# First blocks' exponents from bf16 parts, log a by two loads, and PSUM banks given by hand in a Mamba-2 + ELU kernel

## Chip, cores and metric

One core of a Trainium2 chip runs the whole program in one launch. The metric is the device time in microseconds (us). Before the change it is 388.47 us (median of three runs, 387.79 to 389.34). The profiled execution, from which the trace is read, took 387.49 us, with a span of 385.5 us from the first to the last instruction and a granted TensorE clock of 1.0.

## The reference, cut to what matters

```python
# x (4, 8, 768, 32), a (4, 8, 768), B and C (4, 8, 768, 16): batch, heads, sequence, ...
log_a = np.log(np.clip(a, 1e-06, 1.0))
for c in range(nc):                                  # chunks of 32 along the sequence
    cum = np.cumsum(la, axis=-1)
    L = np.exp(cum[:, :, :, None] - cum[:, :, None, :]) * causal
    M = np.einsum('bhin,bhjn->bhij', Cc, Bc) * L
    y_intra = np.einsum('bhij,bhjd->bhid', M, xc)
    y_inter = np.einsum('bhin,bhnd->bhid', Cc, state) * np.exp(cum)[:, :, :, None]
    y[:, :, sl] = y_intra + y_inter
    Bx = (Bc x xc) * np.exp(cum[:, :, -1:] - cum)    # outer product, cut
    state = np.exp(np.sum(la, axis=-1)) * state + np.sum(Bx, axis=2)

h = x @ w_in                                         # x: y as (3072, 256); w_in (256, 2048)
g = np.where(h > 0.0, h, np.exp(np.minimum(h, 0.0)) - 1.0)
out = g @ w_out                                      # w_out (2048, 256)
```

The weights arrive as 64-bit floats and are turned into 32-bit ones on the chip.

## The kernel before

The kernel takes the sequence in chunks of Q = 64 and works on 12 blocks n = 0 to 11 of 256 positions of one batch. Block 0 and block 1 are the first ones of two batches; from block 4 on two blocks are handled together. For each block the steps are: `turn` (transposes of B and C), `scores` (C times B), the decay L, `weigh` (M = scores times L), `sums` and `states` (the state at each chunk), `across` and `inside` (the two parts of y, copied to yT). Then come eight steps `l1` (y times w_in, two column groups each), each with an `elu`, and eight steps `l2` (times w_out). An fp32 matmul is done in two passes, so one l1 or l2 step is eight passes of 256 columns.

Loads and the exponents of all blocks; rows of `la` are those of block group g = 0, 1, 2 and 0 again:

```python
la = const.tile([P, 2, P], F32, name="la")
for k, g in enumerate((0, 1, 2, 0)):
    (nc.scalar if k % 2 else nc.sync).dma_start(out=la[BH * k:BH * (k + 1)], in_=...)
...
nc.vector.tensor_scalar(out=la, in0=la, scalar1=1e-6, scalar2=1.0, op0=ALU.max, op1=ALU.min)
nc.scalar.activation(la, la, ACT.Ln)
nc.vector.tensor_tensor_scan(out=F[:, 0]..., data0=keep..., data1=la..., ...)   # cum
nc.scalar.activation(F[:, 1], F[:, 0], ACT.Exp)
nc.vector.tensor_tensor(out=E..., in0=<last cum of the chunk>, in1=F_uv, op=ALU.subtract)
nc.scalar.activation(E, E, ACT.Exp)
```

For blocks 0 and 1 the exponent cum[i] - cum[j] is made in PSUM by TensorE: a bf16 product gives the causal mask (`first_low`), fp32 products with 32 rows each add cum[i] (`first_cum`) and subtract cum[j] (`first_minus`), and one exp reads the bank (`first_decay`). Later blocks get cum spread by a DMA through DRAM, and the exp takes -cum as its bias (`decay`), with the mask on GpSimd afterwards.

PSUM has eight banks. Seven are one pool, from which each new tile takes a free one; the eighth is used by the output of l2 and, early, by others:

```python
p_a = ctx.enter_context(tc.tile_pool(name="ps_a", bufs=7, space=PSUM))
p_o = ctx.enter_context(tc.tile_pool(name="ps_o", bufs=1, space=PSUM))
```

A piece of weights (256 columns of two groups) goes through `w_abs` and `w_low` (ScalarE or VectorE), `w_sign`, `w_high_a`, `w_high_b` (VectorE) and `w_sum` (GpSimd). `elu` is two activations and one VectorE operation that frees the bank:

```python
def elu():
    n, i, ps = lag.pop(0)
    nc.scalar.activation(e, ps, ACT.Relu, scale=-1.0)
    nc.scalar.activation(e, e, ACT.Exp, scale=-1.0)
    nc.vector.scalar_tensor_tensor(out=g_of[n][...], in0=e, scalar=1.0, in1=ps,
                                   op0=ALU.subtract, op1=ALU.max)
```

The order at the start and around block 1's end (each engine runs its own part in this order):

```python
first_low(0, 0); first_low(0, 1); idle_products(3); first_cum(*first)
eb = turned(E, "eb", 1.0, nc.scalar); turn(0); first_exp(0); scaled(0, nc.gpsimd); turn_exp(0)
sums(0, pool=p_o, tag="o"); first_minus(*first)
w_abs(0); first_decay(0, 0); w_low(0, nc.scalar); first_decay(0, 1); states(0)
scores(0); w_sign(0); w_high(0); w_sum(0)
for q in range(4): weigh(0, q)
first_low(1, 0); first_low(1, 1, p_o); w_abs(1); w_low(1, nc.scalar)
inside(across(0), 0)
...                                             # second and third piece
l1(0, 0); ...; first_cum(*second); first_minus(*second); l1(0, 1); elu(); ...
first_decay(1, 0); first_decay(1, 1); turn(1); ...; l1(0, 2); elu(); scores(1); sums(1, ...)
...; elu(); states(1); ...; l1(0, 3); w_take(4, nc.vector)
inside(across(1), 1)
ncum = turned(F[0:ROWS, 0], "ncum", -1.0, nc.vector)
w_give(4); elu(); load_bc(3)
for s, (n, i) in enumerate(((1, 0), (1, 1), (0, 4), (1, 2), (0, 5), (1, 3), (0, 6),
                            (1, 4), (0, 7), (1, 5), (1, 6), (1, 7))):
    l1(n, i)
    ...                                         # pieces; decay(2, s - 3) for s = 3 to 6; turn(2)
    if s == 7: scores(2); weigh(2, 0); weigh(2, 1)
    if s == 8: ...; weigh(2, 2); weigh(2, 3); sums(2, pool=p_o, tag="o"); states(2)
    if s == 10: inside(across(2), 2)
    if len(lag) > 1: elu()
```

In the rounds n = 3, 5, 7, 9 of the main loop (m = n + 1 is the pair that is prepared):

```python
for i in range(8):
    l2(n - 2, i); end_of_two(n, 2 * i); l1(n, i)
    while lag: elu()
    if i < 2: decay(m + 1, i + 2); scaled(m + i, nc.gpsimd)
    if i == 2: scores(m, m + 1); sums(m, m + 1); ...   # weigh and states of both
    end_of_two(n, 2 * i + 1)          # inside(across(m, m + 1), m, m + 1) where `ends` says
```

Of the kernel before, what the change touches and what calls it, by code (L numbers as in the profile page):

```python
# [28 lines left out]
def kernel(  # L29
# [33 lines left out]
    ROWS = NG * BH  # L63
# [12 lines left out]
    p_a = ctx.enter_context(tc.tile_pool(name="ps_a", bufs=7, space=PSUM))  # L76
    p_o = ctx.enter_context(tc.tile_pool(name="ps_o", bufs=1, space=PSUM))

    def psum(shape, name):
        return p_a.tile(shape, F32, tag="a", name=name)  # L80
# [6 lines left out]
    la = const.tile([P, 2, P], F32, name="la")  # L87
    for k, g in enumerate((0, 1, 2, 0)):
        (nc.scalar if k % 2 else nc.sync).dma_start(
            out=la[BH * k:BH * (k + 1)],  # L90
            in_=a.rearrange("b h (c s) -> (b h) c s", s=P)[:, 2 * g:2 * g + 2, :])

    nc.scalar.preload_act_table_set("natural_log_exp_and_others")
# [7 lines left out]
    def rows_of(n):  # L101
        b, g = place(n)
        return slice(BH * g + NH * b, BH * g + NH * (b + 1))

    def load_bc(n, c_queue=nc.sync):
        b, g = place(n)
        st.setdefault(n, {})["bc"] = raw.tile([P, 2, 2, NH, N], F32, tag="bc", name="bc")
        for u in range(2):
            sl = slice((2 * g + u) * P, (2 * g + u + 1) * P)
            for k, src in enumerate((B, C)):  # L110
                (nc.sync, c_queue)[k].dma_start(  # L111
                    out=st[n]["bc"][:, k, u], in_=src[b, :, sl, :].rearrange("h s n -> s h n"))
# [26 lines left out]
    def w_load(i):  # L139
        if i < len(pieces):  # L140
            w_raw[i] = conv.tile([P, 2, 2 * CW], U32, tag="w64", name="w64", bufs=W_AHEAD)
            nc.sync.dma_start(out=w_raw[i], in_=pieces[i][1])
# [5 lines left out]
    w_mag = {}  # L148

    def w_words(i):  # L150
        words = w_raw[i].rearrange("p k (f t) -> p k f t", t=2)
        return words[:, :, :, 0], words[:, :, :, 1]

    def w_abs(i):
        w_mag[i] = conv.tile([P, 2, CW], U32, tag="mag", name="mag")
        nc.scalar.activation(w_mag[i].bitcast(F32), w_words(i)[1].bitcast(F32), ACT.Abs)  # L156
# [4 lines left out]
    def w_low(i, eng):  # L161
        if eng is nc.scalar:
            eng.activation(pieces[i][0], w_words(i)[0], ACT.Identity, scale=2.0 ** -51, bias=two)
        else:
            eng.tensor_scalar(
                out=pieces[i][0], in0=w_words(i)[0], scalar1=2.0 ** -51, scalar2=2.0,
                op0=ALU.mult, op1=ALU.add)

    w_sgn = {}

    def w_sign(i):
        w_sgn[i] = conv.tile([P, 2, CW], U32, tag="sgn", name="sgn")
        nc.vector.tensor_scalar(
            out=w_sgn[i], in0=w_words(i)[1], scalar1=0x80000000, scalar2=None,
            op0=ALU.bitwise_and)

    def w_high_a(i):
        mag = w_mag[i]
# [3 lines left out]
            out=mag.bitcast(F32), in0=mag.bitcast(F32),  # L182
# [3 lines left out]
    def w_high_b(i, cols=slice(None)):  # L186
# [5 lines left out]
    def w_high(i):  # L192
        w_high_a(i)
        w_high_b(i)

    def w_sum(i, cols=slice(None)):
# [3 lines left out]
    load_bc(0, nc.scalar)  # L200
    load_x(0)
    w_load(0)
# [3 lines left out]
    idle = att.tile([P, 4, P], BF16, tag="M", name="idle", bufs=8)  # L206
    nc.vector.memset(idle, 0.0)
    ps_idle = p_o.tile([P, 4, P], F32, tag="o", name="ps_idle")

    def idle_products(count):  # L210
        for _ in range(count):
            nc.tensor.matmul(out=ps_idle, lhsT=idle[:, 0], rhs=idle, start=True, stop=True)

    idle_products(7)
# [11 lines left out]
    for v in range(2):  # L226
# [17 lines left out]
    minus = const.tile([P, P], F32, name="minus")  # L244
    nc.gpsimd.tensor_scalar(
        out=minus, in0=ident, scalar1=-1.0, scalar2=None, op0=ALU.mult)

    heads = [const.tile([ROWS, NH, N], F32, name=f"heads{n}") for n in range(3)]
    for n in range(3):
        nc.gpsimd.tensor_copy(  # L250
            heads[n], ident[0:ROWS, rows_of(n)].unsqueeze(2).to_broadcast([ROWS, NH, N]))


    nc.vector.tensor_scalar(out=la, in0=la, scalar1=1e-6, scalar2=1.0, op0=ALU.max, op1=ALU.min)
    nc.scalar.activation(la, la, ACT.Ln)

    F = const.tile([P, 2, 2, P], F32, name="F")
    nc.vector.tensor_tensor_scan(
        out=F[:, 0].rearrange("p c s -> p (c s)"), data0=keep.rearrange("p c s -> p (c s)"),
        data1=la.rearrange("p c s -> p (c s)"), initial=0.0, op0=ALU.mult, op1=ALU.add)  # L260
    nc.scalar.activation(F[:, 1], F[:, 0], ACT.Exp)

    E = const.tile([ROWS, 2, P], F32, name="E")
    F_uv = F[0:ROWS, 0].rearrange("r u (v i) -> r (u v) i", i=Q)
    nc.vector.tensor_tensor(
        out=E.rearrange("r u (v i) -> r (u v) i", i=Q),
        in0=F_uv[:, :, Q - 1:Q].to_broadcast([ROWS, 4, Q]), in1=F_uv, op=ALU.subtract)
    nc.scalar.activation(E, E, ACT.Exp)

# [3 lines left out]
    def write_flat():  # L273
        for v in range(2):
            nc.sync.dma_start(out=flat[v], in_=F[0:ROWS, 0, :, Q * v:Q * v + Q])
        nc.sync.dma_start(out=flat_exp, in_=F[0:ROWS, 1].rearrange("r u i -> r (u i)"))


    def turned(src, name, scale, eng):
        ps = psum([P, 2, ROWS], "ps_" + name)  # L280
        for u in range(2):
            nc.tensor.transpose(out=ps[:, u], in_=src[:, u], identity=ident[0:ROWS, 0:ROWS])
# [552 lines left out]
```

## Time and profile before

| | |
|---|---|
| time, median of 3 | 388.47 us |
| span of the profiled execution | 385.5 us |
| first l1 step starts | 13.68 us |
| last matmul ends | 382.5 us |
| passes of l1 and l2 (L538, L569, L585) | 768, 704 and 64 |
| moved by DMA | 25.15 MB, mean 65 GB/s |

PE is TensorE (PEld its weight loads), DVE VectorE, ACT ScalarE, POOL GpSimd, SP the engine that issues most loads. L538 is line 538 of the kernel: L538 is l1, L569 and L585 l2, L550, L551 and L552 the elu, L397 and L402 the decay, L417 scores, L426 weigh, L445 sums, L462 states, L490 across, L508 inside, L521 the copy to yT, L325 `scaled` (sc = B times eb), L368 and L379 the exponents of the first blocks. In a line of the timeline the first number is the start in us, the second the length of the group, then the operation, its output and inputs, how many instructions it has, and in brackets how long the engine had stood and who ended that. In the row of slices, each digit is the busy share of one fortieth of the span in tenths.

### The profile page before, as it was taken

How to read it: one execution, taken by the hardware profiler on the slowest of the kernel's cores; microseconds unless marked ns; L12 is line 12 of the kernel's file. 1: busy time of each engine (PE TensorE's matmuls, PEld its weight loads, DVE VectorE, ACT ScalarE, POOL GpSimd, SP SyncE). 2: the span in 40 equal slices, each digit the busy share in tenths (PEclk: the TensorE clock that was granted, in tenths of full speed). 3: DMA queues.
4: the chain of work that ended last, by engine and by line, in shares of the span. 5: the costliest groups of instructions: out<-in, count | busy, mean ns of one | idle time of the engine just before them, and what ended most of it. 6: DMA issues, size and time to landing. Idle time of an engine off the chain costs nothing.

```text
span 385.5 us, 8666 instructions
## 1 busy us (share of the span) xinstructions
PE 378.7 (98%) x3544; PEld 324.1 (84%) x3544; DVE 136.9 (36%) x280; ACT 196.7 (51%) x455; POOL 72.1 (19%) x131
## 2 busy tenths in 40 slices
PE   8899999999999999999999999999999999999996
PEld 4678788888888888888888888888888888888885
DVE  4877878932521232611132431123161212221000
ACT  3969969675334576344467335367534333334000
POOL 5525426623200112400022220011310000000000
PEclk9999999999999999999999999999999999999999
DMA  8979956543004505003524002540000000000000
GB/s 173 226 155 263 296 88 148 96 105 94 3 28 57 84 0 138 3 3 61 64 40 136 3 2 41 60 67 29 0 4 2 27 2 23 4 2 28 0 29 27
DMA packets 87176, 25.15 MB, mean 65 GB/s; under 512 B 77312, under 2 KB 81760, under 8 KB 87136
## 3 DMA queue, kind: packets, MB, share of 16 engines
q1 hardware_dynamic: 84960, 24.39, 29.6%
q8 instruction: 28, 0.46, 0.5%
q10 hardware_dynamic: 2176, 0.20, 0.4%
q14 instruction: 12, 0.10, 0.1%
HBM read 21.23 MB, written 3.34 MB: 64 GB/s over the span
## 4 chain that ended last, share of the span: by engine, by line
PE 88%; ACT 4%; DMA 3%; SPq 3%; issue 1%; DVE 0%; ACTq 0%
PE ps_o L569 40%; PE ps_h L538 38%; PE ps_o L585 4%; PE ps_y L508 2%; SPq L111 2%; PE ps_g L417 1%; DMA w<-in_moe_w_in_dram 1%; PE ps_y L490 1%; ACT L L397 1%; DMA xr<-in_x_dram 1%; PE ps_st L445 1%; DMA flat<-F 1%; ACT e L550 1%; SPq L119 1%; ACT mag L156 1%
## 5 line engine op out<-in xcount | busy, mean ns | idle before, releaser
L538 PE MATMUL ps_h<-yT,w_in 128*128 128x256 f32 x768 | 181.4, 380 | 1.4 <-DVE g L552 0.9
L569 PE MATMUL ps_o<-w_out,g 128*128 128x256 f32 x704 | 166.1, 380 | 0.0
L538 PEld LDWEIGHTS ps_h<-yT,w_in 128*128 128x128 f32 x768 | 145.1, 190 | 22.6 <-ACT yT L521 0.9
L569 PEld LDWEIGHTS ps_o<-w_out,g 128*128 128x128 f32 x704 | 132.3, 190 | 18.2 <-POOL L L402 0.2
L552 DVE SCALAR_TENSOR_TENSOR g<-e,ps_h 128x512 f32<-128x512 f32 x96 | 65.9, 686 | 208.3 <-ACT e L551 208.3
L550 ACT ACTIVATE e<-ps_h 128x512 f32<-128x512 f32 x96 | 57.1, 595 | 138.2 <-PE ps_h L538 138.1
L551 ACT ACTIVATE e<-e 128x512 f32<-128x512 f32 x96 | 60.5, 631 | 3.0
L402 POOL TENSOR_SCALAR_AFFINE_SELECT L<-L 64x512 f32<-64x512 f32 x40 | 27.0, 675 | 157.0 <-ACT L L397 155.6
L397 ACT ACTIVATE L<-L,ncum 128x64 f32<-128x64 f32 x160 | 41.8, 333 | 0.0
L521 ACT COPY yT<-ps_y 64x256 f32<-64x256 f32 (+3 forms) x46 | 14.3, 318 | 9.8 <-PE ps_y L508 9.3
L467 POOL TENSOR_TENSOR Sx<-S_new,hmask 128x64 f32<-128x64 f32 x44 | 13.0, 304 | 20.3 <-DVE S_new L462 12.7
L426 DVE TENSOR_TENSOR M<-ps_g,L 128x256 f32<-128x256 f32 x48 | 16.8, 415 | 0.1
L575 ACT COPY ob<-ps_o 128x512 f32<-128x512 f32 x11 | 6.3, 577 | 15.3 <-PE ps_o L569 15.3
L585 PE MATMUL ps_o<-w_out,g 128*128 128x256 f32 x64 | 14.0, 379 | 0.0
L585 PEld LDWEIGHTS ps_o<-w_out,g 128*128 128x128 f32 x64 | 12.2, 190 | 1.7
L198 POOL TENSOR_TENSOR w_in<-mag,w_in 128x512 uint32<-128x512 uint32 x8 | 10.3, 1294 | 15.8 <-DVE mag L188 15.8
L198 POOL TENSOR_TENSOR w_out<-mag,w_out 128x512 uint32<-128x512 uint32 x8 | 10.2, 1275 | 15.4 <-DVE mag L188 15.4
L188 DVE SCALAR_TENSOR_TENSOR mag<-mag,sgn 128x512 uint32<-128x512 uint32 x16 | 12.6, 790 | 0.5
L462 DVE SCALAR_TENSOR_TENSOR S_new<-S_new,ec,ps_st 128x64 f32<-128x64 f32 x40 | 10.9, 279 | 2.1
L156 ACT ACTIVATE mag<-w 128x512 f32<-128x512 f32 x16 | 10.8, 672 | 1.4 <-DMA w<-in_moe_w_in_dram 1.4
L508 PE MATMUL ps_y<-M,xr 64*32 64x64 f32 x768 | 9.6, 225 | 0.0
L342 DVE TENSOR_TENSOR ctm<-ps_tc,hmask 128x512 f32<-128x512 f32 x12 | 8.2, 684 | 3.8 <-PE ps_tc L335 3.8
(66 smaller groups left out, 132.8 us busy)
## 6 DMA issues: line engine op xcount, KB each, us to landing
L<-flat SPq DMA_DIRECT2D x20, 256.0 KB, 4.7
w<-in_moe_w_in_dram SPq DMA_DIRECT2D x8, 512.0 KB, 5.2
w<-in_moe_w_out_dram SPq DMA_DIRECT2D x8, 512.0 KB, 6.0
xr<-in_x_dram SPq DMA_DIRECT2D x24, 128.0 KB, 3.2
out_dram<-ob SPq DMA_DIRECT2D x11, 256.0 KB, 2.2
bc<-in_B_dram SPq DMA_DIRECT2D x24, 64.0 KB, 3.7
bc<-in_C_dram SPq DMA_DIRECT2D x22, 64.0 KB, 3.0
ec<-flat_exp SPq DMA_DIRECT2D x72, 16.0 KB, 1.7
```

The source lines that it names most:

```text
L156: nc.scalar.activation(w_mag[i].bitcast(F32), w_words(i)[1].bitcast(F32), ACT.Abs)
L198: nc.gpsimd.tensor_tensor(out=w, in0=w_mag[i][:, :, cols], in1=w, op=ALU.add)
L397: nc.scalar.activation(L[:, h, u], L[:, h, u], ACT.Exp, bias=ncum[:, u, row:row + 1])
L402: nc.gpsimd.affine_select(out=part, in_=part, pattern=[[0, 4], [0, 2], [1, Q]], compare_op=ALU.is_ge, fill=0.0, base=0, channel_multiplier=-1)
L426: nc.vector.tensor_tensor(out=M, in0=s["g"][q], in1=s["L"][:, 2 * q:2 * q + 2].rearrange("p k u i -> p u k i"), op=ALU.mult)
L508: nc.tensor.matmul(out=y[t][v][col:col + D, at, u], lhsT=s["x"][toks, u, D * h:D * (h + 1)], rhs=s["M"][h // 2][toks, u, h % 2], start=Fal ...
L538: nc.tensor.matmul(out=ps[:, j], lhsT=w_in[:, k, m * P:(m + 1) * P], rhs=yT[n // 2][:, k, n % 2].rearrange("p u i -> p (u i)"), start=(k = ...
L550: nc.scalar.activation(e, ps, ACT.Relu, scale=-1.0)
L551: nc.scalar.activation(e, e, ACT.Exp, scale=-1.0)
L552: nc.vector.scalar_tensor_tensor(out=g_of[n][:, 2 * i:2 * i + 2], in0=e, scalar=1.0, in1=ps, op0=ALU.subtract, op1=ALU.max)
L569: nc.tensor.matmul(out=o_of[n][:, ts], lhsT=g_of[n][:, m, ts * P:(ts + 1) * P], rhs=w_out[:, m], start=(m == 0 and ts == 0), stop=(m == MC ...
L585: nc.tensor.matmul(out=ps, lhsT=g_of[n][:, m, ts * P:(ts + 1) * P], rhs=w_out[:, m], start=(m == 0), stop=(m == MC - 1))
```

## The change

It is meant to shorten the way to the first l1 and to take the first blocks' exponents off TensorE's later work:

- log a is loaded twice. `la0` holds block group 0 four times and comes by one load; all three groups come by a second load and are worked on later, into F and E, whose exps follow still later. The rows of the full table are now batch, head, group.
- cum of the first blocks is split into three bf16 parts in rows 0 to 31, 64 to 95 and 96 to 127 of `cum16`, so that one bf16 product with a selecting column adds all three at once, in place of an fp32 product.
- block 1's exponents move ahead of across(0).
- the first piece of weights is loaded and turned in two halves; the steps of piece 1 move behind inside(0).
- every PSUM bank has a name. The first steps name theirs; the others take the next of seven in turn.
- eb is made twice: a small one for the first blocks, and one for all after `ncum`.
- scores of the pairs 4 and 8 move from step 2 to step 1, and three of the ends move.

```diff
-    p_a = ctx.enter_context(tc.tile_pool(name="ps_a", bufs=7, space=PSUM))
-    p_o = ctx.enter_context(tc.tile_pool(name="ps_o", bufs=1, space=PSUM))
+    banks = ctx.enter_context(tc.tile_pool(name="banks", bufs=1, space=PSUM))
+    ring = [0]
+    def psum(shape, name, bank=None):
+        if bank is None:
+            bank = ring[0]
+            ring[0] = (bank + 1) % 7
+        return banks.tile(shape, F32, tag=f"bank{bank}", name=name)
 ...
+    la0 = att.tile([P, 2, P], F32, tag="M", name="la0", bufs=8)
+    nc.sync.dma_start(out=..., in_=a.rearrange("b h (g t) -> g (b h) t", g=NG)[0:1].to_broadcast([4, BH, BLK]))
+    la = att.tile([ROWS, 2, P], F32, tag="M", name="la", bufs=8)      # loaded on ScalarE's queue
 ...
-    idle_products(7)
+    idle_products(2)                                                   # now fp32
+    log_of(la0)
+    sums_of(F0, la0)
+    nc.scalar.copy(out=cum16, in_=F0[:, 0])
+    from_last(E0, F0[:, 0], nc.vector)
+    nc.scalar.activation(E0, E0, ACT.Exp)
+    nc.vector.tensor_tensor(out=left[low2], in0=F0[low2, 0], in1=cum16[low2], op=ALU.subtract)
+    nc.vector.tensor_copy(cum16[low2], left[low2])
+    nc.vector.tensor_tensor(out=cum16[low3], in0=left[low3], in1=cum16[low3], op=ALU.subtract)
+    nc.scalar.activation(F0[:, 1], F0[:, 0], ACT.Exp)
+    log_of(la)
+    sums_of(F, la)
 ...
+    eb0 = turned(E0, "eb0", 1.0, nc.scalar, BH, 4)
+    turn(0, (5, 6)); first_exp(0, 7); scaled(0, nc.gpsimd); from_last(E, F[:, 0], nc.gpsimd)
+    turn_exp(0); sums(0, bank=(4, 5))
+    for hh in range(2):
+        first_cum(0, hh)
+        first_decay(0, hh)
+    states(0)
+    scores(0, bank=(6, 7, 0, 1))
+    w_abs(0, half[0]); w_low(0, nc.scalar, half[0])
+    weigh(0, 0); weigh(0, 1)
+    w_sign(0, half[0]); w_high(0, half[0]); w_sum(0, half[0])
+    weigh(0, 2); weigh(0, 3)
+    for hh in range(2):
+        first_low(1, hh, 2 + hh)
+        first_cum(1, hh)
+    w_abs(0, half[1]); w_low(0, nc.scalar, half[1])
+    first_decay(1, 0)
+    inside(across(0, bank=(4, 5, 6, 7)), 0)
+    w_sign(0, half[1]); w_high(0, half[1]); w_sum(0, half[1])
+    w_abs(1); w_sign(1); w_high_a(1); w_low(1, nc.scalar); w_sign(2); w_high_b(1); w_sum(1)
+    nc.scalar.activation(F[:, 1], F[:, 0], ACT.Exp)
 ...
-    ncum = turned(F[0:ROWS, 0], "ncum", -1.0, nc.vector)
+    ncum = turned(F[:, 0], "ncum", -1.0, nc.vector, ROWS)
+    nc.scalar.activation(E, E, ACT.Exp)
+    eb = turned(E, "eb", 1.0, nc.scalar, ROWS)
     w_give(4)
     elu()
 ...
-    ends = {(3, 14): 4, (5, 10): 6, (7, 13): 8, (9, 9): 10}
+    ends = {(3, 8): 4, (5, 10): 6, (7, 7): 8, (9, 10): 10}
+    scores_at = {4: 1, 6: 2, 8: 1, 10: 2}
 ...
-                if i == 2:
+                if i == scores_at[m]:
                     scores(m, m + 1)
                     sums(m, m + 1)
```

## The prediction

> **What bounds the kernel now.** I read the busy shares first, then the slices, then the timeline of TensorE, and then, at each place where the change touches TensorE's order, the timelines of the engines that feed it.
>
> ```profile
> PE 378.7 (98%) x3544; PEld 324.1 (84%) x3544; DVE 136.9 (36%) x280; ACT 196.7 (51%) x455; POOL 72.1 (19%) x131
> PE   8899999999999999999999999999999999999996
> ```
>
> TensorE is the bound: 98% busy, and after the second slice never under nine tenths until the last output leaves. In the steady part eight passes (one l1 or one l2 step) follow each other every 1.73 us (92.10 to 93.83 below), 0.216 us a pass. The list of TensorE's waits from 27 us on has only 1.1 us in all (0.9 on g, 0.2 on yT). So there is little to win after 27 us, and every new wait there is paid in full. Only the first 27 us have something to give:
>
> ```profile
> 13.68 1.97 PE L538 MATMUL ps_h<-yT,w_in 128*128 128x256 f32 x8 [0.21 <-ACT yT L521]
> 15.57 1.10 PE L368 MATMUL ps_x<-F,ident 32*64 32x128 f32 x32
> 16.61 1.14 PE L379 MATMUL ps_x<-minus,F 32*128 32x256 f32 x8
> 17.67 1.99 PE L538 MATMUL ps_h<-yT,w_in 128*128 128x256 f32 x8
> ```
>
> The first l1 starts at 13.68 us; then block 1's exponents cost TensorE 2.10 us (15.57 to 17.67) in fp32.
>
> [...] at 10.21 us the exp of block 0 starts only when abs of the weight piece (9.60, waiting for its load) is through. [...] here the two 512-column products of first_low stand 0.25 us apart[...].
>
> **The change, part by part.**
>
> *Start.* One load la0, issued first, replaces four of which VectorE waited for the last (clip at 3.46). Loads of a landed 1.8 to 2.0 us after issue, so the clip can start at 0.79+2.0 = 2.8, 0.65 earlier. Clip 0.32, Ln 0.42, scan 0.69, subtract 0.56, exp 0.42 (all from their rows) put E0 at 5.4 instead of 5.99. But VectorE gets three operations more for the bf16 parts (about 1.2 by the 0.56 of the subtract), the clip and scan of the second load, and ScalarE does Ln of that load (0.42) ahead of the copy of eb: that copy starts at about 6.85, before 6.95. sc and sums come 0.25 earlier (7.75 against 8.02). What was won is mostly given back there.
>
> *Exponents.* Per half block: [...] I take 0.8. Block 0: 7.75+0.4 to 9.75, after which the exps of both halves end at about 10.5. The fourth bank of scores(0) is the one of the second half, so scores(0) ends at 11.1 and the first M starts at 11.2 (11.40 before). Between M1 and M2 VectorE now does the first half of weight piece 0 (about 0.9: half of 0.43+0.43+0.69, and waits), so the last M ends at 13.5 (12.81 before). TensorE does block 1's exponents meanwhile, 2×(0.25+0.8) = 2.1, to 13.2; then across 0.7 and inside 0.8; the copies of yT end at 15.2 (13.87 before): **+1.3**.
>
> *Second piece.* abs of piece 1 now stands behind those copies on ScalarE (it was done at 12.5). From the end of yT: abs 0.6, clamp 0.4, sign of piece 2 0.4, shift 0.7, sum on GpSimd 1.3 = 3.5. So l1(0,1) starts at 18.7 (17.67 before), although the 2.1 us of exponents between are gone. scores(1) then needs the bank of l1(0,1), so its g. I carry **+1.4** to the end of inside(1).
>
> *The ring: first new wait.* Before, a bank came from a pool of free ones; now seven are given in strict turn. The second eb takes one more turn, so l1(1,0) gets the bank of l1(0,3), seven turns back, and waits for its g. ScalarE does that elu after yT, exp of E and the copy of eb.
>
> ```profile
> 26.05 0.88 PE L508 MATMUL ps_y<-M,xr 64*32 64x64 f32 x64
> 26.87 0.39 PE L282 MATMUL ps_ncum<-ident,F 96*128 96x96 f32 x2
> 27.43 11.03 PE L538 MATMUL ps_h<-yT,w_in 128*128 128x256 f32 x48 [0.18 <-ACT yT L521]
> ...
> 26.57 1.64 ACT L521 COPY yT<-ps_y 128x128 f32<-128x128 f32 x6 [2.43 <-PE ps_y L508]
> 28.24 0.60 ACT L550 ACTIVATE e<-ps_h 128x512 f32<-128x512 f32 x1
> 28.86 0.63 ACT L551 ACTIVATE e<-e 128x512 f32<-128x512 f32 x1
> ...
> 29.53 0.69 DVE L552 SCALAR_TENSOR_TENSOR g<-e,ps_h 128x512 f32<-128x512 f32 x1 [0.82 <-ACT e L551]
> ```
>
> Before: l1(1,0) runs from 27.43, pausing for the second half of yT, which is ready at 28.21. After, on the same scale: yT ends 28.21, exp of E 0.42, transposes 0.4, copy 0.3 bring the elu to 29.35; 0.6+0.65 and g 0.7 end at 31.35. Its last six passes ended at 28.27+1.30 = 29.57; now all eight end at 31.35+1.73 = 33.1: **+3.4** (3.5 for TensorE; ScalarE's next wait moves by 3.4). ScalarE is busy nearly without a break from there to 47 us, so nothing is made up.
>
> *The ring: second new wait.* l1(1,5) gets the bank of l1(1,4). Its g stands on VectorE behind the states of block 2:
>
> ```profile
> 46.23 3.72 PE L538 MATMUL ps_h<-yT,w_in 128*128 128x256 f32 x16
> ...
> 47.30 1.30 DVE L462 SCALAR_TENSOR_TENSOR S_new<-S_new,ec,ps_st 128x64 f32<-128x64 f32 x4
> 48.52 0.68 DVE L552 SCALAR_TENSOR_TENSOR g<-e,ps_h 128x512 f32<-128x512 f32 x1
> ...
> 51.59 1.99 PE L538 MATMUL ps_h<-yT,w_in 128*128 128x256 f32 x8 [0.40 <-DVE g L552]
> ```
>
> Before, that pair starts at 46.23; now not before 49.2: 3.0, less the 0.40 wait at 51.59, which goes, and some handover: **+2.5**.
>
> *scores_at.* For the pairs 4 and 8 scores and sums move from step 2 to step 1 of their round. sums needs sc of the second block, which GpSimd makes last, after step 1's elu, four exps and two masks:
>
> ```profile
> 92.10 1.89 PE L569 MATMUL ps_o<-w_out,g 128*128 128x256 f32 x8
> 95.65 1.21 PE L417 MATMUL ps_g<-ctm,bt 32*64 32x128 f32 x64
> 96.78 0.72 PE L445 MATMUL ps_st<-xr,sc 64*32 64x64 f32 x48
> 92.30 0.60 ACT L550 ACTIVATE e<-ps_h 128x512 f32<-128x512 f32 x1 [1.24 <-PE ps_h L538]
> 93.47 1.05 ACT L397 ACTIVATE L<-L,ncum 128x64 f32<-128x64 f32 x4
> 94.58 1.39 POOL L402 TENSOR_SCALAR_AFFINE_SELECT L<-L 64x512 f32<-64x512 f32 x2 [5.26 <-ACT L L397]
> 96.06 0.62 POOL L325 TENSOR_TENSOR sc<-bc,eb 128x256 f32<-128x256 f32 x1
> ```
>
> Step 1's l1 ends at 92.10 and sc at 96.68; sums at 96.78 just missed it. Moved ahead of the l2 at 92.10, scores takes 1.15 and the first block's sums 0.4, to 93.65; TensorE then stands until 96.68: 3.0, twice: **+6.0**. The moved ends (before or after l1 of a later step) meet inputs long ready: 0.
>
> Sum: 388.5 + 1.4 + 3.4 + 2.5 + 6.0 = 401.8; I say 401.5.
>
> **Rivals.** (1) The start wins and the ring costs nothing: the 2.1 us of fp32 exponents go behind other work. For it: their products are bf16 and idle stretches of TensorE before 13 us could hide them. It needs g of l1(0,3) to be ready at 27.4, which the order on ScalarE forbids. It would give 386 to 388. (2) ScalarE becomes a bound that absorbs waits: what TensorE loses at l1(1,0) lets ScalarE and VectorE run ahead, so that the second wait shrinks. Against it: ScalarE can't run ahead of l1, whose results it waits for. It would give about 399. (3) The second load of a lands late behind the C loads and holds VectorE, in order, before ctm: +0.5 to +1. (4) [...]
>
> **Range and chances.** The waits at sc rest on one chain of measured rows (6.0, give or take 0.4), the first ring wait too (3.4, ±0.4); the second may be 1 to 3; the start may be 0.4 to 2.5. That is 398 to 404; for rivals 2 to 4 I widen to 397 to 404.5. Slower by over 2% begins at 396.2, below the range: 0.85. Within 2%: 0.13, if two of these waits are absorbed. Faster by over 2%: 0.02, since the whole start is only 13.7 us.
>
> **What would show it.** TensorE's waits should list g as releaser before l1 at about 33 us and again at about 54, some 3 us each, and sc (GpSimd) before ps_st twice, 3 us each. yT's first copies should end near 15 us, and the first eb copy should start no earlier than 6.5. If TensorE stays without gaps between 90 and 110 us, my reading of the order is wrong, and the time falls by 6. If l1(0,1) starts before 17 us, the start is a gain.

## The result, and the profile after

The changed kernel takes **414.22 us** (413.40 to 415.21, 6 runs) against 388.25 us (387.79 to 389.60) of the kernel before on the same chip: 1.066 times, with a 95% interval of 1.063 to 1.069. Predicted were 401.5 us, 397.0 to 404.5. So the direction was right, and the size was wrong by 12.7 us.

The busy shares, the slices of TensorE and the row of its granted clock, from the page of the kernel after:

```profile
PE 390.1 (94%) x3502; PEld 330.3 (80%) x3502; DVE 139.8 (34%) x288; ACT 198.4 (48%) x462; POOL 73.0 (18%) x135
...
PE   6976979999899999999999979999999999999997
...
PEclk9597898999989999999999989999999999999999
```

TensorE has 42 passes fewer than before (3502 against 3544) and is nevertheless busy 11.4 us longer (390.1 against 378.7): where the granted clock was lower, passes took longer and count as busy for as long (behind the first stand for sc, eight passes of l2 took 3.48 us for the usual 1.89; the clock was 0.50 from 115.28 to 118.60 us). The span grew by 27.5 us (385.5 to 413.0; by the medians it is 26.0), so by an estimate from these two numbers some 16 us (27.5 less 11.4) are new standing and 11 us are the clock. The low slices of the clock (the 2nd, 4th, 5th, 7th, 12th and 24th) stand at or just behind low slices of TensorE; in the page of the kernel before, every slice of that row is a 9.

TensorE's list of waits after (engine, what it wanted, who released it: us in total, times, longest):

```profile
PE ps_st L493 <- POOL sc L381: 7.3, 3, 3.0
PE ps_h L587 <- DVE g L601: 4.5, 2, 2.4
PE ps_eb L335 <- ACT E L310: 2.0, 1, 2.0
PE ps_h L587 <- POOL w_in L212: 1.7, 1, 1.7
PE ps_eb L335 <- ACT E L743: 1.4, 1, 1.4
```

All waits that the prediction named are there: sc (two of 3.0, and one of 1.4 at the start), g (2.4 and 2.1), w_in. The two for E were not foreseen as waits of TensorE: L743 is the exp that the second eb waits for, L310 that of the first block. The latter comes from the start, here in the timeline:

```profile
5.69 0.29 DVE L280 TENSOR_SCALAR la<-la 128x256 f32<-128x256 f32 x1 [4.20 <-DMA la<-in_a_dram]
...
8.12 0.44 PE L335 MATMUL ps_eb<-ident,E 128*128 128x128 f32 x2 [1.96 <-ACT E L310]
...
20.64 1.97 PE L587 MATMUL ps_h<-yT,w_in 128*128 128x256 f32 x8 [0.21 <-ACT yT L570]
24.27 1.99 PE L587 MATMUL ps_h<-yT,w_in 128*128 128x256 f32 x8 [1.66 <-POOL w_in L212]
...
33.74 0.88 PE L557 MATMUL ps_y<-M,xr 64*32 64x64 f32 x64
```

The clip of `la0` starts at 5.69 (3.46 before; 2.8 was predicted), the first l1 at 20.64 (13.68), inside(1) at 33.74 (26.05). The two waits of the ring and that for the exp of E, in the same timeline:

```profile
36.37 0.38 PE L335 MATMUL ps_eb<-ident,E 96*128 96x96 f32 x2 [1.43 <-ACT E L743]
...
39.13 12.77 PE L587 MATMUL ps_h<-yT,w_in 128*128 128x256 f32 x48 [2.38 <-DVE g L601]
...
62.82 5.38 PE L587 MATMUL ps_h<-yT,w_in 128*128 128x256 f32 x16 [2.10 <-DVE g L601]
```

Read the lengths too: 48 passes took 11.03 us before and 12.77 now, 16 took 3.72 and now 5.38. The first stand for sc, and the clock there (columns of the second fence: stretch, its length, busy time, passes, granted clock, DMA share, GB/s):

```profile
111.10 0.43 PE L493 MATMUL ps_st<-xr,sc 64*32 64x64 f32 x24
114.52 0.43 PE L493 MATMUL ps_st<-xr,sc 64*32 64x64 f32 x24 [2.99 <-POOL sc L381]
114.88 3.48 PE L618 MATMUL ps_o<-w_out,g 128*128 128x256 f32 x8
118.15 2.13 PE L587 MATMUL ps_h<-yT,w_in 128*128 128x256 f32 x8
```

```profile
112.00:116.00 4.00, 1.48 (x27) 0.90 0.02 4
116.00:120.00 4.00, 4.00 (x14) 0.67 0.00 0
```

The l2 step behind the stand takes 3.48 us where 1.89 is usual. Where the 27.5 us lie, by marks that both timelines have:

| stretch, to its end | before | after | longer by |
|---|---|---|---|
| start to end of inside(1) | 26.93 | 34.62 | 7.7 |
| to turn(2): exp of E, first ring wait | 38.30 | 51.74 | 5.8 |
| to l1(1,7): second ring wait | 51.59 | 69.36 | 4.3 |
| the two stands for sc, and the rest | | | 9.7 |

### The profile page after: what moved, and what is told of

It reads as the page before. It is cut to its first block, busy times and chain, and to the rows that moved or that the text cites. A ratio compares the mean times of both kernels' runs of the same rounds, so it can differ in the third digit from the quotient of the medians.

```text
span 413.0 us, 8593 instructions
## 1 busy us (share of the span) xinstructions
PE 390.1 (94%) x3502; PEld 330.3 (80%) x3502; DVE 139.8 (34%) x288; ACT 198.4 (48%) x462; POOL 73.0 (18%) x135
## 4 chain that ended last, share of the span: by engine, by line
PE 68%; issue 16%; ACT 6%; DVE 5%; POOL 4%; DMA 1%; POOLq 0%; DVEq 0%; ACTq 0%
PE ps_o L618 29%; PE ps_h L587 29%; PE ps_o L634 3%; POOL L L451 2%; PE ps_y L557 2%; PE ps_y L539 1%; ACT L L446 1%; DMA la<-in_a_dram 1%; ACT e L599 1%; DVE g L601 1%; DVE M L475 1%; PE ps_g L466 1%; POOL sc L381 1%; ACT e L600 1%; PE ps_st L493 1%
## 5 line engine op out<-in xcount | busy, mean ns | idle before, releaser
L587 PE MATMUL ps_h<-yT,w_in 128*128 128x256 f32 x768 | 185.7, 387 | 6.3 <-DVE g L601 4.5
L587 PEld LDWEIGHTS ps_h<-yT,w_in 128*128 128x128 f32 x768 | 148.5, 195 | 28.9 <-issue 5.6
L618 PE MATMUL ps_o<-w_out,g 128*128 128x256 f32 x704 | 169.0, 385 | 0.0
L618 PEld LDWEIGHTS ps_o<-w_out,g 128*128 128x128 f32 x704 | 134.0, 192 | 18.7 <-POOL L L451 0.2
L212 POOL TENSOR_TENSOR w_in<-mag,w_in 128x512 uint32<-128x512 uint32 (+1 forms) x9 | 10.4, 1155 | 25.6 <-DVE mag L202 21.2
L634 PE MATMUL ps_o<-w_out,g 128*128 128x256 f32 x64 | 14.0, 379 | 0.0
L212 POOL TENSOR_TENSOR w_out<-mag,w_out 128x512 uint32<-128x512 uint32 x8 | 10.2, 1275 | 20.2 <-DVE mag L202 20.2
L634 PEld LDWEIGHTS ps_o<-w_out,g 128*128 128x128 f32 x64 | 12.2, 190 | 1.7
L493 PE MATMUL ps_st<-xr,sc 64*32 64x64 f32 x352 | 5.4, 231 | 7.7 <-POOL sc L381 7.3
L202 DVE SCALAR_TENSOR_TENSOR mag<-mag,sgn 128x512 uint32<-128x512 uint32 (+1 forms) x17 | 11.9, 699 | 0.5
L493 PEld LDWEIGHTS ps_st<-xr,sc 64*32 64x32 f32 x352 | 3.8, 110 | 10.0 <-POOL sc L381 8.4
L169 ACT ACTIVATE mag<-w 128x512 f32<-128x512 f32 (+1 forms) x17 | 10.8, 638 | 0.0
```

The lines of the kernel that those rows point to most:

```text
L212: nc.gpsimd.tensor_tensor(out=w, in0=w_mag[i][:, :, cols], in1=w, op=ALU.add)
L493: nc.tensor.matmul(out=ps[v][32 * q:32 * q + 32, at, u], lhsT=s["sc"][toks, u, 2 * q:2 * q + 2].rearrange("p h n -> p (h n)"), rhs=s["x"][ ...
L587: nc.tensor.matmul(out=ps[:, j], lhsT=w_in[:, k, m * P:(m + 1) * P], rhs=yT[n // 2][:, k, n % 2].rearrange("p u i -> p (u i)"), start=(k = ...
L618: nc.tensor.matmul(out=o_of[n][:, ts], lhsT=g_of[n][:, m, ts * P:(ts + 1) * P], rhs=w_out[:, m], start=(m == 0 and ts == 0), stop=(m == MC ...
L634: nc.tensor.matmul(out=ps, lhsT=g_of[n][:, m, ts * P:(ts + 1) * P], rhs=w_out[:, m], start=(m == 0), stop=(m == MC - 1))
```

## The experiments

The times are medians; the kernel before ran beside them at 387.7 to 388.5 us. Where the median of a run and its trace differ, the stretches are read from the trace.

### The start: why is la0 late?

**c_later**: C of block 0 is issued later, so that fewer packets run beside la0.

```diff
-    load_bc(0, nc.scalar, (0,))
     nc.scalar.preload_act_table_set("natural_log_exp_and_others")
-    load_bc(0, nc.scalar, (1,))
+    load_bc(0, nc.scalar)
```

> The changed kernel with both C loads of block 0 issued behind the table load, as before the change; la0 stays one load that reads its rows four times. Theory A (the 64-byte packets of C, now issued at 0.79 us on the other queue, hold la0 up): the clip of la0 starts at about 3.2 us instead of 5.69, TensorE keeps its full clock through the start, the first l1 starts at about 15 to 16 us instead of 20.64, and the time falls by about 5 us to 409. Theory B (one load of 128 rows with a repeated source is slow by its form): the clip stays at 5.5 or later and the time stays within 1 us of 414.2.

Measured: 413.98 us; the clip at 5.46, the first l1 at 20.23. The packets of C are not the cause: other runs with this load unchanged have the clip at 5.2 to 5.7.

**la_four**: la0 by four loads of 32 rows, as the kernel before loads a.

```diff
-    nc.sync.dma_start(out=la0..., in_=a.rearrange("b h (g t) -> g (b h) t", g=NG)[0:1].to_broadcast([4, BH, BLK]))
+    for k in range(4):
+        (nc.scalar if k % 2 else nc.sync).dma_start(
+            out=la0[BH * k:BH * (k + 1)]..., in_=a.rearrange("b h (g t) -> g (b h) t", g=NG)[0])
```

> The changed kernel with la0 brought by four loads of 32 rows, two on each queue, ahead of everything, as before the change; C follows at once on ScalarE's queue. Theory B (form of the load): the clip starts at 3.5 us, the first l1 at 15.5, the time falls by 5 us to 409. Theory A (C's packets in front): also about 3.5, since la0 is now ahead of C on both queues; this run alone doesn't tell them apart, with the other it does. A third theory, that the start matters little because the second weight piece holds l1(0,1) anyway: the clip moves to 3.5 but the time falls by less than 2.

Measured: 411.14 us (ratio to before 1.058 to 1.061), 3.1 less than the changed kernel. VectorE and TensorE in its timeline:

```profile
3.58 0.29 DVE L281 TENSOR_SCALAR la<-la 128x256 f32<-128x256 f32 x1 [2.08 <-DMA la<-in_a_dram]
...
15.59 2.09 PE L588 MATMUL ps_h<-yT,w_in 128*128 128x256 f32 x8 [0.21 <-ACT yT L571]
19.22 1.99 PE L588 MATMUL ps_h<-yT,w_in 128*128 128x256 f32 x8 [1.54 <-POOL w_in L213]
```

The first l1 is 5 us earlier, and the clock stays at 1.00 from 5 to 28 us. Of these 5 us some are lost again: at inside(1) TensorE stands 1.27 us for nothing that the profile names (more on this under fill_half).

**la_two** and **la_x**: two broadcast loads of 64 rows, one on each queue; and one load of 128 different rows, from x in place of a, so that its exponents and output have other values and only its times count.

```diff
 # la_two
+    for k, queue in enumerate((nc.sync, nc.scalar)):
+        queue.dma_start(out=la0[2 * BH * k:2 * BH * (k + 1)]..., in_=...[0:1].to_broadcast([2, BH, BLK]))
 # la_x
-        in_=a.rearrange("b h (g t) -> g (b h) t", g=NG)[0:1].to_broadcast([4, BH, BLK])
+        in_=x.rearrange("b h (g t) d -> (b h g) (t d)", t=8)[0:P]
```

> The changed kernel with la0 by two broadcast loads of 64 rows, one on each queue. Theory A (a load that repeats rows of DRAM is what is slow): as late as with one load, the clip at 5 to 5.7. Theory B (the size of one load sets when it lands: one of 128 KB lands 4.3 to 4.9 us after issue, four of 32 KB 1.8 to 2.0): between, 2.5 to 3.5 us after issue, the clip at 3.5 to 4.5.

> The changed kernel, but la0 holds 128 different rows of 1 KB from x in place of four times the same 32 rows of a: one load of the same size with nothing repeated (exponents and output are then other values; the instructions are the same). Theory A (the repetition is slow): lands 2 to 2.5 us after issue, clip near 3. Theory B (one load of 128 KB is slow): 4.3 to 4.9, clip at 5.3 to 5.7, and the time stays at 414.

Measured, one run each: 411.7 and 411.1 us. The clip of la_two, then of la_x:

```profile
6.26 0.29 DVE L281 TENSOR_SCALAR la<-la 128x256 f32<-128x256 f32 x1 [4.77 <-DMA la<-in_a_dram]
```

```profile
3.15 0.29 DVE L280 TENSOR_SCALAR la<-la 128x256 f32<-128x256 f32 x1 [1.66 <-DMA la<-in_x_dram]
```

The size is not the cause: 128 KB in one load land 2.3 us after issue, when nothing is repeated. Two loads of half the size with repetition are later still than the whole. Four plain loads of the same 32 rows land after 1.8 to 2.1, so the source itself may be read four times.

**la_turned**: still one load that repeats its source, but with the 32 rows as the outermost dimension and the 4 copies inside. Row 4r + k of `la0` then holds row r, so its output has other values and only its times count.

```diff
-        in_=a.rearrange("b h (g t) -> g (b h) t", g=NG)[0:1].to_broadcast([4, BH, BLK])
+        in_=a.rearrange("b h (g t) -> g (b h) t", g=NG)[0].unsqueeze(1).to_broadcast([BH, 4, BLK])
```

> The changed kernel with la0 still one load that repeats its source four times, but with the repetition inside: the slowest dimension of the source is the 32 rows, not the 4 copies, so row 4r + k of la0 holds row r of a (exponents and output are then of mixed rows; the instructions are the same). Theory A[...]: lands as early as la_x, 2.2 to 2.6 us after issue, clip at 3.1 to 3.5. Theory B (repeated reading is slow in whatever order): 4.3 to 4.7, clip at 5.2 to 5.7.

Measured: 409.95 us (1.050 to 1.061), 4.3 less than the changed kernel. It landed 2.7 us after issue:

```profile
3.51 0.29 DVE L280 TENSOR_SCALAR la<-la 128x256 f32<-128x256 f32 x1 [2.02 <-DMA la<-in_a_dram]
```

So it is the place of the repeated dimension, and not the repetition: with 4 copies outermost the clip starts at 5.69, with 2 at 6.26, with 32 rows outermost at 3.51. Why the place counts is not shown: no view tells how a load was carried out.

### The ring

**bank_list**: the banks that have no name come from a written list, in the order in which the pool of the kernel before gave them out; the second eb takes bank 7.

```diff
-            bank = ring[0]
-            ring[0] = (bank + 1) % 7
+            if plan:
+                bank = plan.pop(0)             # 2, 3, 0, 6, 5, 4, 2, 1, 0, 5, ...
+            else:
+                bank = turns[ring[0]]          # 5, 3, 6, 1, 4, 2, 0
+                ring[0] = (ring[0] + 1) % 7
-    eb = turned(E, "eb", 1.0, nc.scalar, ROWS)
+    eb = turned(E, "eb", 1.0, nc.scalar, ROWS, 7)
```

> The changed kernel with the banks of all unnamed tiles up to block 3 given by a list, the one that the pool chose before the change, and from then on in the same cyclic order; the second eb takes bank 7. Theory 1 (the strict turn makes l1(1,0) wait for g of l1(0,3) and l1(1,5) for g of l1(1,4)): both waits for g (2.4 and 2.1 us) go, the wait of eb for the exp of E (1.4) stays, the time falls by 4.5 if gaps cost their length, by 7 to 8 with the clock's drops behind them. Rival (ScalarE or VectorE is the bound there and the banks only show it): the waits move to another l1 and the time falls by less than 2.

Measured: 404.5 us (ratio 1.038 to 1.044), 9.7 less. The waits for g are back to the 0.46 and 0.40 us of the kernel before; the wait of 1.42 for the exp of E is still there. In its trace the stretch to turn(2) is 4.8 us shorter than in the changed kernel, the next one 4.3.

**eb_own**: only the last line of that edit; the ring stays.

> The changed kernel, but the second eb goes into bank 7 and takes no turn of the ring. l1(1,0) then comes seven turns after another tile than l1(0,3), and its wait for g (2.38 us in the trace, before it 1.43 for the exp of E) loses its cause; the distance from l1(1,5) to l1(1,4) is not changed by it. Theory A (each ring wait has a cause of its own): the first goes, the second of 2.1 us stays: 414.2 less 4 to 5 (2.0 of standing, the rest clock), 409 to 410. Theory B (the second wait is an echo of the first, since the engines behind it are shifted): both go, 405 as with the list of banks.

Measured: 407.89 us (1.049 to 1.055), 6.3 less. The first wait for g is gone, the second is unchanged, so each has a cause of its own:

```profile
57.59 5.38 PE L587 MATMUL ps_h<-yT,w_in 128*128 128x256 f32 x16 [2.10 <-DVE g L601]
```

Not all of the 6.3 us is the ring. In the traces the end of inside(1) comes 2.1 us earlier (32.48 for 34.62), in a part that the edit doesn't touch: `la0` happened to land earlier (clip at 5.32), and the half clock at the start lasted 3.4 us in place of 10.2. The stretch from there to turn(2) is 3.1 us shorter, and the next one is the same (17.6). So the first wait is worth 3.1 us here and 4.8 in bank_list, where no slow clock followed the exp of E; the second, with the slow clock behind it, 4.3.

### The stands for sc, and the clock

**scores2**: `scores_at` is 2 for all pairs; the moved ends stay.

> The changed kernel with scores of the pairs 4 and 8 back at step 2. Theory 1 (a gap costs its length): the two waits of sums on sc of 3.0 us each go, the time falls by 6.0 to 408.2. Theory 2 (a gap of 3 us also halves TensorE's clock for some 3.4 us): the l2 behind each gap, 3.4 us for eight passes, goes back to 1.9, and the time falls by 9.5 to 404.7.

Measured: 404.6 us (1.040 to 1.048), 9.6 less. Two stands of 3.0 are only 6.0 of it. That the slow clock behind them is the rest doesn't follow from this run alone: part of the 9.6 lies elsewhere (its half clock at the start lasted 3.4 us, and none came behind the second ring wait), and across(8), whose end now follows its sums closely, costs 1.4 us that are new (shown under all_three). From l1(1,7) to the end of the trace it is 8.1 us shorter than the changed kernel; with these 1.4 that is 9.5, against 9.7 for the two places in the table above.

**fill** and **fill_half**: 12 and 6 products more, whose results nobody reads, between the sums of the first and of the second block of these pairs.

```diff
         for at, n in enumerate(ns):
+            if at and scores_at[ns[0]] == 1:
+                for _ in range(12):            # fill_half: 6, fill_third: 3
+                    nc.tensor.matmul(out=free, lhsT=w_out[:, 0, 0:P], rhs=w_out[:, 0], start=True, stop=True, ...)
```

> The changed kernel, with 12 more products of 128 by 256 (0.216 us each, 2.6 us) of the weights, whose results nobody reads, between the sums of the first and of the second block of the pairs 4 and 8, that is where TensorE stood 3.0 us for sc. The wait itself stays, as sc comes no sooner; only the standing still goes. Theory A (a gap costs its own length and then some 3.4 us at half the clock, 1.7 us more): the two gaps give back 2 x 1.7, 410.8, and the clock of the stretches 116 to 120 and 240 to 244 is 1.00. Theory B (the slow clock after a gap only delays work that other engines would have delayed anyway): 414, whatever the clock shows. If the whole 9.6 us that scores2 won came from something other than wait and clock, the result says nothing of A and stays near 414 as well.

Measured: 420.76 us, against 410.8 and 414 of the theories. A mistake of mine: such a product is two passes (the trace has 24 passes for the 12), so they took 5.45 us at the first place, 2.4 more than the gap. Its time decides nothing about the clock.

> As fill, but with half as many products: in fill each product of 128 by 256 was two passes of 0.216 us, so its 12 took 5.4 us where 2.6 were meant, 2.4 us more than the gap of 3.0 they fill. Now 6 products, 12 passes, 2.6 us. Theory A (a gap costs its length and then 1.7 us of slow clock): 414.2 - 2 x 1.7 = 410.8, with the granted clock at 1.00 through both places. Theory B (the slow clock costs nothing of its own): 414.

Measured: 413.86 us (1.062 to 1.070). The clock did what theory A says (the l2 step behind takes 2.00 us, for 3.48), but the time didn't fall. TensorE's timeline, then the clock:

```profile
110.09 2.86 PE L496 MATMUL ps_st<-w_out 128*128 128x256 f32 x12
113.15 0.43 PE L502 MATMUL ps_st<-xr,sc 64*32 64x64 f32 x24 [0.20 <-POOL sc L381]
...
123.25 1.49 PE L566 MATMUL ps_y<-M,xr 64*32 64x64 f32 x127
126.29 0.24 PE L566 MATMUL ps_y<-M,xr 64*32 64x64 f32 x1 [1.54 <-issue]
```

```profile
112.00:116.00 4.00, 3.80 (x41) 1.00 0.00 0
116.00:120.00 4.00, 4.00 (x20) 1.00 0.00 0
```

In the last product of inside(4) there is a new stand, whose releaser is "issue", that is, nothing that the profile shows; 1.61 us at inside(8) too. Together they take 3.2 us, about what the clock gave back. In the list of transfers a block of 16 KB (the only packet from 123 to 125 us) starts at 123.9 on the queue that the profile calls "instruction", in the middle of the 192 short products of across and inside; TensorE stands from 124.74 to 126.29. That the one is the cause of the other is not shown.

**scores1**: so that no instruction is added, the kernel before with `scores_at` 1 for the pairs 4 and 8 and with the moved ends, nothing else.

```diff
-    ends = {(3, 14): 4, (5, 10): 6, (7, 13): 8, (9, 9): 10}
+    ends = {(3, 8): 4, (5, 10): 6, (7, 7): 8, (9, 10): 10}
+    scores_at = {4: 1, 6: 2, 8: 1, 10: 2}
...
-                if i == 2:
+                if i == scores_at[m]:
```

> The kernel before with one part of the change alone: scores_at 1 for the pairs 4 and 8, and the moved ends; nothing of the start, of the loads and of the banks. Theory A (a stand of 3.0 us for sc, then 1.7 us of slow clock, twice, whatever the rest of the kernel does): 388.3 + 2 x 4.7 = 397.7. Theory B (only the stand counts, as the prediction had it): 388.3 + 6.0 = 394.3. No instruction is added or taken away[...].

Measured: 401.48 us against 387.66 of before: 1.031 to 1.040, 13.8 longer. In its timeline:

```profile
97.17 0.43 PE L445 MATMUL ps_st<-xr,sc 64*32 64x64 f32 x24 [2.98 <-POOL sc L325]
97.53 3.53 PE L569 MATMUL ps_o<-w_out,g 128*128 128x256 f32 x8
...
108.96 1.20 PE L508 MATMUL ps_y<-M,xr 64*32 64x64 f32 x97
111.61 0.46 PE L508 MATMUL ps_y<-M,xr 64*32 64x64 f32 x31 [1.45 <-issue]
```

The stands are 2.98 and 2.94; the two steps after the first take 3.53 and 2.08, those after the second 3.78 and 2.83, where 1.89 is usual: 1.8 and 2.8 for the clock. Two stands without releaser (1.45 and 1.32) make 2.8. Together 13.3, of 13.8 measured (14.7 in this trace). Again a 16 KB block started on the queue "instruction" at 109.36, 0.8 us before the stand began and 2.2 before it ended. Theory B (394.3) falls; theory A (397.7) is short as well, by the stands without releaser and the longer slow clock behind the second stand.

**fill_third**: 3 products, so that half of each stand is left.

> The changed kernel with 3 products (6 passes, 1.3 us) in each of the two stands for sc, so that 1.7 us of each stand are left. In fill_half the clock stayed at 1.00 through both places, but at the next inside TensorE stood 1.54 and 1.61 us with no releaser[...]. Theory A (clock 1.7 us a gap, and a gap of 1.7 us does not lower it[...]): stands without releaser of 0 to 0.5 us, clock 1.00, 411 to 411.5. Theory B (the clock drop costs nothing, the stands are a delay that was always there): 414.

Measured: 409.7, 409.9 and 412.7 us (ratio 1.055 to 1.066), and 416.1 in a fourth run, so the time alone decides little. The stands left are 1.50 and 1.46, and the clock stays up:

```profile
112.00:116.00 4.00, 4.00 (x20) 1.00 0.00 0
116.00:120.00 4.00, 4.00 (x70) 1.00 0.00 0
```

Of the two stands without releaser, expected at 0 to 0.5 us each, the first fell to 0.63 and moved into l1, the second stayed at 1.68 in inside(8).

### What is left without the new waits?

**all_three**: la_four, bank_list and scores2 at once.

> The changed kernel with the three repairs at once: la0 by four loads (3.1 won alone), the banks by the list (9.7 alone), scores of all pairs at step 2 (9.6 alone). Theory A (separate causes at separate places, which add): 414.2 - 22.4 = 391.8, and what is left over the kernel before is the later start (1.9 at the first l1, 1.5 for the second piece of weights) and the wait for the exp of E (1.4, less what before waited there). Theory B (part of each gain is the same clock or is given back): 394 or more.

Measured: 393.17 us (1.010 to 1.016). The sum of the three was 391.8: they add, within 1.4 us. Its trace is 5.9 us longer than that of the kernel before. inside(1) ends at 28.49, 1.6 later than before. The wait for the exp of E is 1.43 and is followed by slow passes (48 take 12.18 us, 1.15 over the 11.03 of before). The last part is at pair 8: with scores at step 2 again but its end still moved ahead, across(8) comes one pair of steps behind sums and waits for Sx, the states masked on GpSimd:

```profile
228.22 1.10 PE L547 MATMUL ps_y<-cts,Sx 32*64 32x64 f32 x48 [0.52 <-POOL Sx L523]
```

across(8) and inside(8) take 3.74 us there (226.94 to 230.68) and 2.37 in the kernel before (232.91 to 235.28), 1.4 more. Together that is some 5.5 of the 5.9 us. scores2, best, best2 and best3 keep this end too.

**best**, **best2**, **best3**: three further orders of the start. best puts abs of pieces 0 and 1 early and the second log behind piece 1; best2 puts it behind l1(0,2); best3 into the places where ScalarE and VectorE stood in best2, and gives block 1's exponents other banks.

```diff
 # best, the core
+    w_abs(0)
     for hh in range(2):
         first_cum(0, hh)
         first_decay(0, hh)
...
-    scores(0, bank=(6, 7, 0, 1))
+    scores(0, bank=(6, 7, 2, 3))
...
+    w_abs(1)
     inside(across(0, bank=(4, 5, 6, 7)), 0)
...
+    log_of(la)                                # best2 and best3: after l1(0, 2)
+    sums_of(F, la)
```

> all_three, and the start put in another order: the first piece of weights whole, its abs ahead of the exponents' exps as in the kernel before; clip, Ln and scan of the second load of a moved behind the work of piece 1, so that VectorE and ScalarE come to eb, ctm and cts sooner; scores(0) in banks that wait for no exp; abs of piece 1 ahead of yT; the exp of E ahead of inside(1). Theory A (what was left in all_three is the order on VectorE and ScalarE, and block 1's exponents can lie where TensorE stands for them): first l1 at 13.7 to 14.2, l1(0,1) without 2.1 us of exponents ahead of it at 16 to 16.5, and 387 to 389, at most 1 us better than before. Theory B (the chain of the weight pieces through VectorE and GpSimd sets the pace of l1(0,1) and l1(0,2), whatever TensorE has to do): 388 to 391, with waits for w_in where the exponents were.

Measured: 390.0 us (1.004 to 1.007), within theory B. As it says, TensorE waits for pieces of weights where the exponents were (2.0 us in all); the longest of these waits:

```profile
20.73 1.99 PE L593 MATMUL ps_h<-yT,w_in 128*128 128x256 f32 x8 [1.28 <-POOL w_in L220]
```

> As best, but the second load of a is worked on only after l1(0,2): Ln, scan, the two exps and the writing of flat come behind the third piece of weights, so that abs of piece 2 follows yT at once, as in the kernel before (in best it came at 17.44, in the kernel before at 13.74, and TensorE waited 2.0 us in all for pieces of w_in). Theory A (the order on ScalarE and VectorE was all that kept the bf16 exponents from paying): l1(0,2) near 19, the end of inside(1) 1 to 1.6 us ahead of before (26.93), 386.8 to 387.5. Theory B (ScalarE has 1.7 us more to do in the first 27 us, for the copy to bf16, the second Ln and two more exps, and has no room for it): 388 to 389.5, with waits for w_in or for g and L in its place.

Measured: 395.52 us (1.016 to 1.023), outside both theories. I had given block 1's exponents a bank that VectorE still had to read (1.89 us of TensorE, for M). That is part of the 7 us; TensorE also waits for g (2.2 in three waits), Sx (1.9 in two) and E (0.8).

> As best2, with its own new wait taken away: there block 1's exponents took bank 7, which weigh(0, 1) had not yet read (1.89 us of TensorE for M). Here they have the banks 0 and 1, and Ln, scan and exps of the second load lie in the places where ScalarE and VectorE stood in best2 (between elu(0,1) and elu(0,2), and after it). Theory A (then the bf16 exponents pay): end of inside(1) at 26 to 27 (26.93 before), 387 to 388.3. Theory B (the second log, the copy to bf16 and two more exps on ScalarE cost what they win): 388.5 to 390.

Measured: 395.47 us (1.018 to 1.022), again outside both. Up to inside(1) it is the closest order to before: inside(1) ends at 27.29 against 26.93. But log a is now written out later, and block 2's L comes back later. ScalarE, in order, stands for it with the elu behind it; then TensorE stands for g. ScalarE, then TensorE:

```profile
39.34 1.06 ACT L452 ACTIVATE L<-L,ncum 128x64 f32<-128x64 f32 x4 [5.58 <-DMA L<-flat]
```

```profile
42.41 4.00 PE L593 MATMUL ps_h<-yT,w_in 128*128 128x256 f32 x16 [2.74 <-DVE g L607]
```

No order that I tried is faster than the kernel before. All three carry the 1.4 us of across(8); best without it would be near 388.6 (an estimate, 390.0 less 1.4), level with the kernel before.

## Why the prediction was wrong, point by point

- **What bounds it**: right. TensorE was full, and each new wait was paid in full, most of them with a slow clock on top.
- **Start, +1.4 at the end of inside(1)**: 7.7. The step that failed first is "Loads of a landed 1.8 to 2.0 us after issue, so the clip can start at 0.79+2.0 = 2.8": that was read from four plain loads and carried over to one whose outermost dimension is 4 copies, for which the clip started 4.9 after issue (0.79 to 5.69). TensorE then stood 1.96 us, and its clock was 0.50 to 0.53 from 9.5 to 20 us. With a load that lands early the rest of the step holds: la_turned has l1(0,1) at 18.96 (18.7 predicted), all_three ends inside(1) 1.6 later than before (1.4 predicted). That is luck in part: sums starts at 8.77 in la_turned, 1.0 later than the 7.75 predicted, and the exponents make up for some of it, with 0.67 us per half block in place of 0.8, which was an estimate that no trace of the kernel before showed. Two small readings in that step were off without changing its sum: the five parts of the second piece make 3.4 us and not 3.5, and the two products of first_low start 0.30 us apart at 4.2 us and 0.23 at 10.1, not 0.25.
- **First ring wait, +3.4**: 5.8 in the trace. Cause and releaser were right (eb_own shows the cause). The stand was 1.43 + 2.38 = 3.8 less the short waits of before; the rest is the clock, 12.77 - 11.03 = 1.7.
- **Second ring wait, +2.5**: 4.3. The stand was 2.1, and the 16 passes behind it took 1.7 more. This drop doesn't always come. Behind the same 2.10 us these 16 passes took 3.69 us in six traces (scores2, fill, fill_half, fill_third, la_two, la_turned) and 5.38 in five (the changed kernel, c_later, la_four, la_x, eb_own); six of these are sorted below.
- **scores_at, +6.0**: the two stands measured 2.99 and 2.96, the step itself was exact. With the clock the two places cost 9.7 (the table).
- **Rival 4, a slower clock at the new gaps, was true, and I left it out of the sum**: this is the second step that failed, the clock behind each new wait. What I allowed for it was an estimate that no trace of the kernel before showed (its clock was 1.00 throughout). The slower clock cost 1.7 us at both ring waits and 1.8 to 2.8 at the stands for sc (scores1), and at the start it was 0.50 for 10.2 us. Of rival 1 nothing is left; rival 2 did not occur, as eb_own shows for the second wait; rival 3 found the wrong load: la0 itself was the late one.
- **Left out**: the exp of E that the second eb waits for (1.43). I counted it in ScalarE's chain for the elu only, not on TensorE's own way. With the ring wait behind it this costs nothing more, as both end with the same g; without the ring wait it stays (bank_list, all_three).
- **The moved ends, 0**: right for the changed kernel. With scores back at step 2 one of them costs 1.4 (all_three).

Summed: the terms as measured, 7.7 + 5.8 + 4.3 + 9.7, are 27.5 against my 13.3. The late load and what it set off is 6, the clock at the other four places some 7.

The clock's record in the trace of the changed kernel shows when the slow clock came. It was 0.50 from 9.41 us for 10.24 us, from 36.71 for 6.83, and from 64.02, 115.22 and 241.51 for 3.41 each. These lengths are 3, 2, 1, 1 and 1 times 3.413 us, and the starts lie 8, 8, 15 and 37 times 3.413 us apart. Laid through such a stretch, marks 3.413 us apart also sort the second ring wait in the six traces whose clock shows where they lie, to about 0.1 us (the marks of the other five traces are worked out from the mean clock of their stretches, which makes them estimates):

| run | stand of 2.10 us for g | marks | the 16 passes behind it |
|---|---|---|---|
| changed kernel | 60.72 to 62.82 | 60.6 and 64.0, around it | 5.38 us |
| c_later | 60.34 to 62.44 | 59.9 and 63.3, around it | 5.38 us |
| la_four | 56.84 to 58.94 | 56.1 and 59.5, around it | 5.38 us |
| eb_own | 55.49 to 57.59 | 55.4 and 58.8, around it | 5.38 us |
| scores2 | 59.04 to 61.14 | 59.2, inside it | 3.69 us |
| fill | 58.38 to 60.48 | 58.7, inside it | 3.69 us |

First the changed kernel, then scores2, each from one mark to the next and on to the one after it (TensorE alone; columns as above):

```profile
60.60:64.00 3.40, 1.30 (x23) 1.00 0.81 236
64.00:67.40 3.40, 3.40 (x10) 0.50 1.04 137
```

```profile
59.20:62.60 3.40, 1.46 (x7) 1.00 1.05 271
62.60:66.00 3.40, 3.40 (x108) 1.00 0.94 107
```

So in these six traces it went with the moment whether this wait cost 2.1 or 3.8 us; what lies behind the marks is not shown. It may be part of why six runs of the changed kernel spread from 413.4 to 415.2 us; that isn't shown either. The stands for sc all show the slow clock: the sixteen of 2.94 to 3.00 us, two in each of eight traces (the changed kernel, c_later, la_four, la_two, la_x, bank_list, eb_own, scores1), were all followed by an l2 step of 3.11 to 3.78 us, for 1.89. Shorter ones differ: 1.43 us before the second eb were followed by a slow clock in all_three (0.72 from 28 to 34 us), 1.42 in bank_list were not (1.00 from 28 to 40), nor were the 1.5 in fill_third (1.00 from 112 to 120).

Still open: how much standing it takes, since stands of the same 1.4 us differ, and what makes TensorE stand where the profile names no releaser. The times of the 16 KB blocks in fill_half and scores1 fit, but no run changed these transfers alone.

## What to carry to other kernels

A stand of 3 us on a TensorE that was otherwise full cost its length and then, in the changed kernel and in scores1, 1.8 to 2.8 us of half clock; one of 2.1 us did so (1.7) in five of eleven traces. Count it so, and look at the row of the granted clock before calling a wait small. Don't carry a load's landing time over from another form of load; one with 4 copies as its outermost dimension took 4.9 us here, with 32 rows outermost 2.7. And when banks are given by hand, the turn must follow the order in which readers free them: one tile more in a strict ring made a wait of 2.38 us seven turns later.

## What was unexpected of the hardware

- Loads of the same 128 KB landed 1.8 to 4.9 us after issue, by their form: four plain ones 1.8 to 2.1, one without repetition 2.3, one with the copies inside 2.7, one with them outermost 4.4 to 4.9 (by the start of the clip).
- The clock dropped after the stands of 3.0 us: in the changed kernel it was 0.50 for 3.41 us behind each, and the eight passes of l2 took 3.48 and 3.36 us, for 1.89. After 2.10 us the next 16 passes took 5.38 us in five traces and 3.69 in six.
- TensorE stood 1.0 to 1.9 us with no releaser, thirteen times in nine traces, twelve of them among the 64x64 products of inside. In fill_half, with 12 passes more ahead of inside(4) than in the changed kernel, such a stand of 1.54 us is there, and the changed kernel has none. For three of them (one in fill_half, two in scores1) the transfers show a 16 KB block that started on the queue "instruction" 0.8 to 1.1 us before the stand and 2.2 to 2.5 us before its end. Such blocks also came without a stand: 27 packets (0.44 MB) on that queue in the changed kernel.
